# Spreading a batch's preparation between half tiles of attention, a joint gate product, and a plain first layer for the fifth expert

## The chip, the cores and the metric

The kernel runs on one core of a Trainium2 chip. The metric is the device time of one execution in microseconds. The time before is the median of three runs.

## The reference

An attention without softmax is followed by a mixture of experts with balanced capacity.

```python
kv  = einsum('bhsd,bhse->bhde', k, v)          # 8 batches, 8 heads, 576 rows, 64 columns
out = einsum('bhsd,bhde->bhse', q, kv)
x   = out / sqrt(mean(out*out, -1) + 1e-6) * g_norm   # then to (4608, 512)
logits = x @ w_gate                            # 8 experts
# greedy: pairs (token, expert) in falling order of logit, 576 tokens for each expert
h = maximum(x[mask] @ w1[e], 0)                # 512 -> 1024
out[mask] = h @ w2[e]                          # 1024 -> 512
```

Everything is float32. Which tokens an expert gets is only known once all logits are there and the search for the cut has run.

## The kernel before, in words

**Attention.** Eight batches run one after the other. `prepare(b)` is a generator that makes a batch ready: it multiplies k and v (`kv_ps`, L326), turns q with TensorE transposes (`turn_q`, L312, four at a time into `qt`), adds the two halves of the product (`odd`, L332 on ScalarE, then `kv`, L334 on VectorE), and joins to each head's 64 x 64 product 8 columns that give the gate's logits (`kvx`). For the gate it transposes `kv` (`t_ps`, L345), copies it out of PSUM (`kvt`, L347, ScalarE), multiplies it with the scaled gate weights (`w_ps`, L353, once for each half of the partitions) and copies the result into `kvx` (L355). At its end it issues the six loads of the batch after the next (L87, on SP's queue, paced to three under way).

`tiles()` works through a batch in tiles of 128 rows, four for an even batch and five for an odd one. A tile is 8 products in 16 instructions (`o_ps`, L388), two evictions on ScalarE (`sq` L394, `o_sb` L395) and a sum on VectorE (`ms`, L396). At the end of a batch the norm is worked out, the logits go to `lg` and GpSimd scales the rows (`xo`, L415), which SP writes out to `x_dram`.

The order on TensorE, VectorE, ScalarE and SP is that of the program (`manual_schedule`). A loop takes one part of `prepare(b + 1)` after each tile of batch b, and whatever is left after the last tile but one or the last. `prepare` has five parts: kv product of head pair 0 with a turn, the same for pair 1, pairs 2 and 3 together with the additions, turn and `kvt`, and turn, `w_ps`, turn and loads. `early_piece()` puts pieces of the expert search's opening work on VectorE beside the tiles. The transposes, `t_ps` and `w_ps` share two PSUM buffers (tag `tr`); `o_ps` has two of its own.

**Experts.** The eight experts are served one after the other, t = 0 to 7. While expert t is computed, VectorE searches for the tokens of the next ones (`threshold`, `assign`, `fetch`, `control`). The generator `layers(t)` yields the estimated TensorE time of each product, and a loop counts it down to decide where the search's next piece goes. `fetch(t)` isn't started before expert t - 2 is done.

The second layer always uses seven products of quarter matrices in place of eight, with sums made on GpSimd (`column_sums` L915, `sums` L929). For the first layer there are two ways. The plain one (L951) does 64 products with `xt` and `w1`. The other, `first_layer` (L894), does seven products for eight too; it needs sums of weights on GpSimd (`unit_sums`, L855), sums of tokens on VectorE (`token_sums`, L842), and additions of partial results on VectorE (L868, L872). Which experts take it is a tuple:

```python
BOTH = (E - 4, E - 3, E - 2, E - 1)
both = t + 1 in BOTH
turns = {(n, 7) for n in range(1, 6)} if both else {(6, 6)} if t == 0 else {(6, 3)}
```

`turns` says where in the second layer of expert t the tokens of expert t + 1 are transposed (L815): all five blocks there if t + 1 is in `BOTH`; otherwise two there and three in the plain first layer that follows.

Of the kernel before, what the change touches and what calls it, by code (L numbers as in the profile page):

```python
# [7 lines left out]
FT = mybir.dt.float32  # L8
# [7 lines left out]
P = 128  # L16
# [9 lines left out]
def kernel(  # L26
# [272 lines left out]
    def prepare(b):  # L299

        k_sb, v_sb = loaded.pop(("k", b)), loaded.pop(("v", b))

        q_sb = loaded.pop(("q", b)).rearrange("p r j d -> p (r j d)")
        NT = NP * R // 2
        qt = att.tile([P, 2, NT, HP], FT, name="qt", tag="qt", bufs=3)
        turned_q[b] = qt

        def turn_q(n):
            m = min(4, NT - 4 * n)
            t_ps = psa.tile([P, 4, P], FT, name="qt_ps", tag="tr", bufs=2)  # L310
            for x in range(m):
                nc.tensor.transpose(t_ps[:, x, :], q_sb[:, (4 * n + x) * P:(4 * n + x + 1) * P], ident)  # L312

            to, got = qt[:, :, 4 * n:4 * n + m], t_ps[:, 0:m].rearrange("p x (l c) -> p l x c", l=2)
            if n in (1, 2):
                nc.vector.tensor_copy(to, got)
            else:
                nc.scalar.copy(to, got)


        kv_ps = psa.tile([P, 2, 512], FT, name="kv_ps", tag="kv")
        for r in range(NP):
            for j in range(R):
                for l in range(2):
                    ls, cs = slice(l * D, (l + 1) * D), slice(j % 2 * D, (j % 2 + 1) * D)
                    nc.tensor.matmul(kv_ps[cs, l, r * D:(r + 1) * D], lhsT=k_sb[ls, r, j, :], rhs=v_sb[ls, r, j, :],  # L326
                                     start=(j < 2), stop=(j >= R - 2))
            if r < 2:
                turn_q(r)
                yield  # L330
        odd = att.tile([D, 2, NP * D], FT, name="odd", tag="odd")
        nc.scalar.copy(odd, kv_ps[D:P, :, 0:NP * D])  # L332
        kv = att.tile([D, NP, 2, D], FT, name="kv", tag="kv")
        nc.vector.tensor_tensor(kv.rearrange("p r l d -> p l r d"),  # L334
                                kv_ps[0:D, :, 0:NP * D].rearrange("p l (r d) -> p l r d", d=D),
                                odd.rearrange("p l (r d) -> p l r d", d=D), op=AL.add)

        kvx = att.tile([P, H, W], FT, name="kvx", tag="kvx", bufs=3)
        for n in range(2):
            nc.gpsimd.tensor_copy(kvx[n * D:(n + 1) * D, :, 0:D], kv.rearrange("p r l d -> p (r l) d"))  # L340
        yield
        turn_q(2)
        t_ps = psa.tile([P, NP, D], FT, name="t_ps", tag="tr", bufs=2)
        for r in range(NP):
            nc.tensor.transpose(t_ps[:, r, :], kv[:, r].rearrange("p l d -> p (l d)"), ident[0:D, 0:D])  # L345
        kvt = att.tile([P, NP, D], FT, name="kvt", tag="kvt")
        nc.scalar.copy(kvt, t_ps)  # L347
        yield
        turn_q(3)
        w_ps = psa.tile([P, NP, 2 * E], FT, name="w_ps", tag="tr", bufs=2)  # L350
        for r in range(NP):
            for n in range(2):
                nc.tensor.matmul(w_ps[n * D:(n + 1) * D, r], lhsT=kvt[:, r, :],  # L353
                                 rhs=gw[:, r].rearrange("p l e -> p (l e)"), start=True, stop=True)
        nc.vector.tensor_copy(kvx[:, :, D:W], w_ps.rearrange("p r (l e) -> p (r l) e", l=2))  # L355
        kv_of[b] = kvx
        turn_q(4)
        if b + 2 < B:
            for h in range(2):
                for name in "kvq":  # L360
                    load(name, b + 2, h)
# [5 lines left out]
    def tiles(c0, rows):  # L367


        T = len(rows)  # L370
        o_sb = att.tile([P, T, H, W], FT, name="o_sb", tag="o_sb", bufs=2)
        xo = att.tile([P, T, H, D], FT, name="xo", tag="xo", bufs=LAG + 1)
        ms = att.tile([P, T * H], FT, name="ms", tag="ms")
        for t, halves in enumerate(rows):


            o_ps = psa.tile([P, 2, 512], FT, name="o_ps", tag="o", bufs=2)
            for r2 in range(NP // 2):
                for l in range(2):
                    for rp in range(2):  # L380
                        r = 2 * r2 + rp
                        at = [slice(h * HP, (h + 1) * HP) for h in range(2)]
                        parts = [(slice(0, P), halves[0], 2)] if halves[0][0] == halves[1][0] else [
                            (at[n], half, 1) for n, half in enumerate(halves)]
                        for rows_at, (bn, j), m in parts:
                            block = R * r + j
                            ks = slice(block % 2 * D, (block % 2 + 1) * D)
                            nc.tensor.matmul(  # L388
                                o_ps[rows_at, rp, (2 * r2 + l) * W:(2 * r2 + l + 1) * W],
                                lhsT=turned_q[bn][ks, l, block // 2:block // 2 + m].rearrange("p x c -> p (x c)"),  # L390
                                rhs=kv_of[bn][ks, 2 * r + l], start=True, stop=True)
            o4 = o_ps[:, :, 0:NP * W].rearrange("p b (h w) -> p b h w", w=W)
            sq = att.tile([P, H, D], FT, name="sq", tag="sq")
            nc.scalar.activation(sq.rearrange("p (b h) d -> p b h d", b=2), o4[:, :, :, 0:D], ACT.Square, scale=D ** -0.5)  # L394
            nc.scalar.copy(o_sb[:, t].rearrange("p (b h) w -> p b (h w)", b=2), o_ps[:, :, 0:NP * W])  # L395
            nc.vector.reduce_sum(out=ms[:, t * H:(t + 1) * H], in_=sq, axis=AXX)  # L396
            yield
        rt = att.tile([P, T * H], FT, name="rt", tag="rt")
        nc.scalar.activation(rt, ms, ACT.Sqrt, bias=eps)
        inv = att.tile([P, T * H], FT, name="inv", tag="inv")  # L400
        nc.vector.reciprocal(inv, rt)

        nc.vector.scalar_tensor_tensor(rt, in0=inv, scalar=-0.5, in1=inv, op0=AL.mult, op1=AL.mult)
        nc.vector.scalar_tensor_tensor(rt, in0=ms, scalar=EPS, in1=rt, op0=AL.add, op1=AL.mult)
        nc.vector.scalar_tensor_tensor(inv, in0=rt, scalar=1.5, in1=inv, op0=AL.add, op1=AL.mult)  # L405
        part = att.tile([P, T * H, E], FT, name="part", tag="part")
        nc.vector.tensor_tensor(
            part, o_sb[:, :, :, D:W].rearrange("p t h e -> p (t h) e"),
            inv.rearrange("p (a o) -> p a o", o=1).to_broadcast([P, T * H, E]), op=AL.mult)
        nc.vector.reduce_sum(out=lg[:, :, c0:c0 + T].rearrange("p e t -> p t e"),  # L410
                             in_=part.rearrange("p (t h) e -> p t e h", t=T), axis=AXX)

        for t in range(T):
            if c0 + T <= last_own:
                nc.gpsimd.tensor_tensor(xo[:, t], o_sb[:, t, :, 0:D],  # L415
                                        inv[:, t * H:(t + 1) * H].rearrange("p (h o) -> p h o", o=1).to_broadcast([P, H, D]),
                                        op=AL.mult)
            else:
                for h in range(H):
                    late.append(lambda t=t, h=h: nc.scalar.mul(xo[:, t, h], o_sb[:, t, h, 0:D],  # L420
                                                               inv[:, t * H + h:t * H + h + 1]))
        for x in range(0, T, 2):
            y = min(x + 2, T)
            writes.append(lambda x=x, y=y: paced(nc.sync.dma_start(
                x_dram[(c0 + x) * P:(c0 + y) * P, :].rearrange("(t p) f -> p t f", p=P),
                xo[:, x:y].rearrange("p t h d -> p t (h d)"))))
# [21 lines left out]
    with tc.manual_schedule(engines={PE, DVE, ACTE, SPE}):  # L448
# [2 lines left out]
        for _ in range(12):  # L451
            nc.tensor.matmul(w_ps, lhsT=ones_b, rhs=wide, start=True, stop=True)
        for n, _ in enumerate(prepare(0)):
            if n == 2:
                scale_gate()
        bound_logits()
        for b in range(B):
            parts = prepare(b + 1) if b + 1 < B else iter(())
            n = 0
            tile_work = work(b)  # L460
            for _ in tile_work:
                next(parts, None)
                early_piece()
                n += 1
                if n == 4 + b % 2 and b + 1 < B:
                    for _ in parts:
                        pass
            while b + 2 >= B and earlies:
                early_piece()
            for do in late:  # L470
# [358 lines left out]
    FH, TH, DH = FC // 2, (NB - 1) // 2 * P, DM // 2  # L829


    BOTH = (E - 4, E - 3, E - 2, E - 1)
    sums_of = {}

    def token_sums(t):
# [275 lines left out]
```

## Time and profile before

| | us |
|---|---|
| median of 3 runs | 683.48 |
| lowest and highest | 682.77, 684.42 |
| the profiled execution | 683.48 |
| its span | 681.3 |
| PE busy in the span | 624.6 |
| DVE busy in the span | 451.7 |
| ACT, POOL busy | 173.8, 336.2 |
| mean granted TensorE clock | 0.938 |

PE is TensorE, PEld its weight loads, DVE VectorE, ACT ScalarE, POOL GpSimd, SP the queue that issues the loads. The page cuts the span into 40 slices of 17 us; in its rows of digits each one is a tenth (9 is 90% or more), and PEclk is the clock granted to TensorE. In a table of stages each row is a stretch, its length, the busy time and number of instructions of each engine, the clock, the share of the DMA engines and GB/s. In a list of waits a row says who waited for whom, the total in us, how often, and the longest. A `ps` in a name is a PSUM tile.

The attention takes the stretch up to about 121 us, the first search runs from there to 160 us, and the experts from 166 us to the end.

### The profile page before, as it was taken

The numbers are of one execution on the slowest core, as the hardware profiler recorded it, in microseconds if no ns is written. First come the engines' busy times: TensorE is split into PE (matmuls) and PEld (weight loads), VectorE is DVE, ScalarE is ACT, GpSimd is POOL, SyncE is SP. The second block draws the span as 40 slices with busy tenths as digits, with TensorE's granted clock in tenths as the row PEclk, the third lists the DMA queues.
The fourth block names the chain that finished last, engine by engine and source line by source line (L and its number), as shares of the span: only waits on it lengthen the run. The fifth ranks groups of instructions, "written<-read, shape, count | busy, mean of one in ns | idle before, by whom it ended". The sixth has DMA issues, their size and how long they took to land.

```text
span 681.3 us, 12850 instructions
## 1 busy us (share of the span) xinstructions
PE 624.6 (92%) x4994; PEld 487.5 (72%) x4995; DVE 451.7 (66%) x1449; ACT 173.8 (26%) x372; POOL 336.2 (49%) x335
## 2 busy tenths in 40 slices
PE   6999998337999999999999999987989999999994
PEld 4887877233878777877786788656857867786882
DVE  4436778887788888898888786788884056233311
ACT  1436666701210221022102211221113113212200
POOL 1024545002544456355607572785289659938622
PEclk8559999557999999999999999999999999999998
DMA  8978998306307306225207404700190334001001
GB/s 277 307 254 282 310 307 336 150 17 198 118 1 273 111 4 241 76 70 212 106 0 246 142 2 148 232 8 0 46 322 20 125 121 142 1 15 55 1 0 69
DMA packets 41404, 91.02 MB, mean 134 GB/s; under 512 B 3456, under 2 KB 3456, under 8 KB 41344
## 3 DMA queue, kind: packets, MB, share of 16 engines
q1 hardware_dynamic: 34752, 71.31, 30.2%
q0 software_dynamic: 5888, 18.88, 8.3%
q8 instruction: 39, 0.64, 0.4%
q14 instruction: 21, 0.17, 0.1%
q10 hardware_dynamic: 704, 0.02, 0.1%
HBM read 71.32 MB, written 18.87 MB: 132 GB/s over the span
## 4 chain that ended last, share of the span: by engine, by line
PE 76%; DVE 11%; POOL 3%; issue 3%; DMA 3%; ACT 2%; POOLq 0%; DVEq 0%; ACTq 0%; SPq 0%
PE y_ps L1001 27%; PE h_ps L951 17%; PE h_ps L894 9%; PE o_ps L388 5%; PE kv_ps L326 3%; PE y_ps L1016 3%; PE qt_ps L312 3%; PE t_ps L815 3%; DMA k_sb<-in_k_dram 2%; PE given_ps L538 1%; PE given_ps L534 1%; POOL tw L915 1%; PE warm_ps L690 1%; POOL out_dram L822 1%; DMA out_dram<-y_sb,outs 1%
## 5 line engine op out<-in xcount | busy, mean ns | idle before, releaser
L951 PE MATMUL h_ps<-xt,w_sb 128*128 128x256 f32 (+1 forms) x512 | 133.8, 412 | 0.1
L951 PEld LDWEIGHTS h_ps<-xt,w_sb 128*128 128x128 f32 x512 | 93.9, 190 | 25.8 <-issue 3.1
L1001 PE MATMUL y_ps<-tw,sh 128*128 128x256 f32 x384 | 87.4, 381 | 0.0
L1001 PEld LDWEIGHTS y_ps<-tw,sh 128*128 128x128 f32 x384 | 71.4, 190 | 8.9
L742 POOL DMA_INDIRECT xg<-x_dram,ids x40 | 38.2, 956 | 67.4 <-DVE held_ps L658 40.0
L929 POOL TENSOR_TENSOR sh<-hid 128x512 f32<-128x512 f32 x32 | 40.6, 1269 | 52.1 <-ACT hid L954 34.6
L818 ACT ACTIVATE xt<-t_ps,g_col 128x512 f32<-128x512 f32 (+1 forms) x40 | 25.8, 646 | 144.0 <-PE t_ps L815 113.0
L1001 PE MATMUL y_ps<-w_sb,hid 128*128 128x256 f32 x256 | 57.8, 381 | 3.4 <-DVE u L872 3.4
L264 DVE TENSOR_TENSOR over<-mx,held_ps 128x1152 bf16<-128x1152 f32 x42 | 56.9, 1354 | 1.6 <-DVE held_ps L269 0.2
L1001 PEld LDWEIGHTS y_ps<-w_sb,hid 128*128 128x128 f32 x256 | 48.1, 190 | 10.8 <-DVE u L872 3.9
L822 POOL DMA_INDIRECT out_dram<-y_sb,outs x32 | 33.2, 1038 | 43.0 <-DVE u L971 20.7
L894 PE MATMUL h_ps<-sx,tv 128*128 128x288 f32 x192 | 53.1, 410 | 1.0 <-POOL tv L855 0.7
L954 ACT ACTIVATE hid<-h_ps 128x256 f32<-128x256 f32 (+1 forms) x64 | 26.3, 411 | 104.0 <-PE h_ps L951 99.7
L869 ACT ACTIVATE hid<-hid 128x288 f32<-128x288 f32 x64 | 28.2, 445 | 89.1 <-DVE hid L868 86.4
L415 POOL TENSOR_TENSOR xo<-o_sb,inv 128x512 f32<-128x512 f32 x31 | 33.0, 1095 | 28.6 <-DVE inv L405 20.6
L978 POOL TENSOR_TENSOR y_sb<-u,u 128x512 f32<-128x512 f32 x8 | 10.1, 1269 | 72.7 <-issue 49.3
L388 PE MATMUL o_ps<-kvx,qt 64*128 64x72 f32 (+1 forms) x640 | 44.6, 297 | 1.3 <-ACT o_sb L395 1.2
L915 POOL TENSOR_TENSOR tw<-w_sb 128x512 f32<-128x512 f32 x32 | 40.0, 1272 | 11.2 <-DMA w_sb<-in_moe_w_dram 11.0
L388 PEld LDWEIGHTS o_ps<-kvx,qt 64*128 64x128 f32 (+1 forms) x640 | 39.0, 202 | 7.0 <-issue 3.8
L894 PEld LDWEIGHTS h_ps<-sx,tv 128*128 128x128 f32 x192 | 35.8, 190 | 11.2 <-POOL tv L855 1.6
L580 DVE SCALAR_TENSOR_TENSOR held_ps<-n_full,held_ps 32x64 f32<-32x64 f32 x168 | 37.7, 224 | 5.8
L894 PE MATMUL h_ps<-xt,w_sb 128*128 128x288 f32 x128 | 37.1, 412 | 2.8 <-DVE hid L868 2.8
(230 smaller groups left out, 1107.9 us busy)
## 6 DMA issues: line engine op xcount, KB each, us to landing
w_sb<-in_moe_w_dram SPq DMA_DIRECT2D x16, 1024.0 KB, 6.1
w_sb<-in_moe_w_dram SPq DMA_DIRECT2D x8, 2048.0 KB, 16.2
k_sb<-in_k_dram SPq DMA_DIRECT2D x16, 576.0 KB, 5.4
v_sb<-in_v_dram SPq DMA_DIRECT2D x16, 576.0 KB, 6.0
q_sb<-in_q_dram SPq DMA_DIRECT2D x16, 576.0 KB, 6.8
x_dram<-xo SPq DMA_DIRECT2D x16, 512.0 KB, 3.8
x_dram<-xo SPq DMA_DIRECT2D x4, 256.0 KB, 4.1
xg<-x_dram,ids POOLq DMA_INDIRECT x40
```

What stands on the lines that cost most here:

```text
L264: nc.vector.tensor_tensor(over[:, c0:c1], mx[:, c0:c1].rearrange("p (c o) -> p c o", o=1).to_broadcast([P, c1 - c0, NCAND]), cand[:, 1:NCA ...
L388: nc.tensor.matmul(o_ps[rows_at, rp, (2 * r2 + l) * W:(2 * r2 + l + 1) * W], lhsT=turned_q[bn][ks, l, block // 2:block // 2 + m].rearrange ...
L415: nc.gpsimd.tensor_tensor(xo[:, t], o_sb[:, t, :, 0:D], inv[:, t * H:(t + 1) * H].rearrange("p (h o) -> p h o", o=1).to_broadcast([P, H, D ...
L580: nc.vector.scalar_tensor_tensor(some[g * QP:(g + 1) * QP], in0=n_full.to_broadcast([QP, 2 * QP]), scalar=0.5, in1=one_more, op0=AL.is_gt, ...
L742: tokens = nc.gpsimd.indirect_dma_start(out=xg[0:nr], out_offset=None, in_=x_dram, in_offset=bass.IndirectOffsetOnAxis(ap=ids[0:nr, n:n + ...
L822: put = nc.gpsimd.indirect_dma_start(out=out, out_offset=bass.IndirectOffsetOnAxis(ap=ids_of[t][0:nr, n:n + 1], axis=0), in_=y_sb[0:nr, :] ...
L869: nc.scalar.activation(hid[:, f, cs], hid[:, f, cs], ACT.Relu)
L894: nc.tensor.matmul(p_ps, lhsT=left[:, d], rhs=right[:, d], start=d == 0, stop=d == 1)
L915: in_order(nc.gpsimd.tensor_tensor(o[:, m:m + 2], x[:, m:m + 2], y[:, m:m + 2], op=AL.subtract))
L929: in_order(nc.gpsimd.tensor_tensor(o[:, ms], x[:, ms], y[:, ms], op=op))
L951: nc.tensor.matmul(h_ps, lhsT=w1[:, 2 * (d % 2) + d // 2, f * P:(f + 1) * P], rhs=xt[:, d, cs], start=(d == 0), stop=(d == DC - 1))
L1001: nc.tensor.matmul(p_ps[:, n], lhsT=left[:, f, n * P:(n + 1) * P], rhs=right[:, f], start=(f == 0), stop=(f == FH - 1))
```

## The change

`prepare` gets seven parts: head pairs 2 and 3 are parted, and the last turn with the loads stands by itself. A tile yields after its first half too, so that parts can go between halves: at steps 0, 1, 2, 3, 5, 6, 7 of eight in an even batch and at 0, 1, 3, 4, 6, 8, 9 of ten in an odd one. `early_piece` is still called once for each tile. For the gate, `kvt` is copied twice side by side (one buffer instead of two), so that one product gives both halves of the partitions. And expert t = 4 is taken out of `BOTH`: its first layer is the plain one.

```diff
@@ prepare
             if r < 2:
                 turn_q(r)
+            if r + 1 < NP:
                 yield
...
-        kvt = att.tile([P, NP, D], FT, name="kvt", tag="kvt")
-        nc.scalar.copy(kvt, t_ps)
+        kvt = att.tile([P, NP, 2, D], FT, name="kvt", tag="kvt", bufs=1)
+        nc.scalar.copy(kvt, t_ps.rearrange("p r (o d) -> p r o d", o=1).to_broadcast([P, NP, 2, D]))
         yield
         turn_q(3)
         w_ps = psa.tile([P, NP, 2 * E], FT, name="w_ps", tag="tr", bufs=2)
         for r in range(NP):
-            for n in range(2):
-                nc.tensor.matmul(w_ps[n * D:(n + 1) * D, r], lhsT=kvt[:, r, :],
-                                 rhs=gw[:, r].rearrange("p l e -> p (l e)"), start=True, stop=True)
+            nc.tensor.matmul(w_ps[:, r], lhsT=kvt[:, r].rearrange("p n d -> p (n d)"),
+                             rhs=gw[:, r].rearrange("p l e -> p (l e)"), start=True, stop=True)
         nc.vector.tensor_copy(kvx[:, :, D:W], w_ps.rearrange("p r (l e) -> p (r l) e", l=2))
         kv_of[b] = kvx
+        yield
         turn_q(4)
@@ tiles
+                if r2 == 0:
+                    yield
@@ the loop over batches
         for n, _ in enumerate(prepare(0)):
-            if n == 2:
+            if n == 4:
                 scale_gate()
...
-            n = 0
-            tile_work = work(b)
-            for _ in tile_work:
-                next(parts, None)
-                early_piece()
-                n += 1
-                if n == 4 + b % 2 and b + 1 < B:
-                    for _ in parts:
-                        pass
+            for n, _ in enumerate(work(b)):
+                if n in ((0, 1, 3, 4, 6, 8, 9) if b % 2 else (0, 1, 2, 3, 5, 6, 7)):
+                    next(parts, None)
+                if n % 2:
+                    early_piece()
+            for _ in parts:
+                pass
@@ experts
-    BOTH = (E - 4, E - 3, E - 2, E - 1)
+    BOTH = (E - 3, E - 2, E - 1)
```

## The prediction

> **What bounds the kernel now.** I read the page's head first, then its slices, then stages.
>
> ```profile
> span 681.3 us, 12850 instructions
> ...
> PE 624.6 (92%) x4994; PEld 487.5 (72%) x4995; DVE 451.7 (66%) x1449; ACT 173.8 (26%) x372; POOL 336.2 (49%) x335
> ...
> PEclk8559999557999999999999999999999999999998
> ```
>
> PE is busy 92% of the span, so time is won by less PE work, fewer PE waits, or a faster PE clock. The third line shows that the clock is not always full: slices 2 and 3 (17 to 51 us) run at half of it although PE never rests there. That is the attention, whose batches I cut out of the PE timeline by their first o_ps product: batch 0 takes 19.15 to 37.94 us (18.8), batch 1 to 55.31 (17.4), then 11.4, 11.8, 11.4, 12.2 and 11.6 us for batches 2 to 6. The first two do the same work, at half clock.
>
> Next, the experts. Stages cut at the first h_ps and y_ps products: the third expert's second layer is the row from 332.34, the fourth's two layers the next two, then the fifth's two (the one whose first layer the change rewrites starts at 428.18).
>
> ```profile
> 332.34:362.62 30.28, 30.28 (x177) 23.75 (x176) 26.24 (x91) 2.98 (x5) 8.24 (x7) 1.00 0.03 10
> 362.62:397.32 34.70, 34.70 (x193) 26.55 (x194) 28.81 (x105) 8.58 (x19) 22.44 (x20) 1.00 0.54 182
> 397.32:428.18 30.86, 30.86 (x171) 24.39 (x170) 20.80 (x62) 4.73 (x8) 16.21 (x17) 1.00 0.26 95
> 428.18:465.58 37.40, 30.27 (x157) 21.92 (x156) 33.59 (x110) 7.54 (x18) 26.10 (x26) 1.00 0.32 99
> ```
>
> Columns: stretch, its length, busy PE, PEld, DVE, ACT, POOL, then clock and DMA. The fifth expert's first layer is the only one here with PE idle: 37.40 long, 30.27 busy. DVE is busy 33.59 of it. Who held PE, in that stretch and in the attention (19 to 121 us):
>
> ```profile
> PE y_ps L1001 <- DVE u L872: 3.4, 1, 3.4
> PE h_ps L894 <- DVE hid L868: 1.2, 2, 0.9
> PE given_ps L538 <- DVE over L264: 1.1, 2, 0.7
> ...
> PE qt_ps L312 <- ACT kvt L347: 2.0, 4, 0.5
> PE qt_ps L312 <- DVE kvx L355: 1.2, 3, 0.4
> PE o_ps L388 <- ACT o_sb L395: 1.2, 2, 0.8
> ```
>
> So DVE, which does the search and the seven-product layer's additions together, bounds the fifth expert's first layer. The attention loses only 3.2 us to the gate's chain; its clock costs far more.
>
> [...] from shares of half clock in 1.7 us stretches, the flips fall at 9.66, 13.05, 19.9 and 50.6 us, distances of 1, 2 and 9 windows of 3.41. [...] The busy table cut at those windows, all of PE:
>
> ```profile
> 9.66:13.07 3.41, 3.41 (x48) 0.50 1.02 371
> ...
> 19.90:23.31 3.41, 3.41 (x54) 0.50 0.94 314
> ...
> 43.79:47.21 3.42, 3.42 (x52) 0.50 0.91 309
> 47.21:50.62 3.41, 3.41 (x84) 0.50 0.31 113
> 50.62:54.03 3.41, 3.41 (x66) 1.00 0.56 184
> ```
>
> All are full, yet only the first and the 47.21 one were followed by full clock. The same table for the kv_ps products (L326) alone:
>
> ```profile
> 9.66:13.07 3.41, 1.49 (x40) 0.50 1.02 371
> 19.90:23.31 3.41, 1.33 (x36) 0.50 0.94 314
> 26.73:30.14 3.41, 1.27 (x46) 0.50 0.87 262
> 30.14:33.55 3.41, 1.13 (x38) 0.50 0.95 341
> 43.79:47.21 3.42, 1.33 (x36) 0.50 0.91 309
> 47.21:50.62 3.41, 2.32 (x72) 0.50 0.31 113
> ```
>
> [...] A block of 16 o_ps products (one tile, 1.91 us cold) seems to count little[...]. That is my reading, not a shown fact.
>
> **The change part by part.**
>
> *Expert 5 (index 4) goes back to the plain first layer.* PE: removed 7 x 4 x 2 products of 288 columns, the same as the last expert's, 27.4 us (616.25 to 643.61). Added 64 products in 128 instructions: 64 at 216 ns (16 take 3.46) and 64 at 275 ns (16 take 4.40), 31.4 us. So PE work grows by 4.0. DVE loses 16 x 455 + 12 x 452 ns = 12.7 us there and 4 x 0.75 of sx in the stage ahead; POOL loses 16 x 0.73 = 11.7. The stage becomes 30.27 + 4.0 = 34.3 against 37.40: -3.1. Second way: two turning transposes instead of five stay in the layer ahead, so the pair becomes what the third and fourth experts show, 30.28 + 34.70 = 64.98, against 30.86 + 37.40 = 68.26: -3.3. I take -3.2, bounds -4.2 and -2. The search can't run further ahead: its fetch waits until the previous expert is done, so the sixth expert's start, with its own wait of 1.9 us, stays.
>
> *Gate's part.* 16 w_ps instructions (0.64 us) become 8 with weights of 128 columns, at the o_ps price (1.05/16 = 66 ns) 0.53: -0.1 for each of 8 batches, -0.9. kvt's copy doubles to 512 columns: 384 to about 590 ns, the qt row's mean. ACT is 7.2 of 11.4 us busy, so the 0.2 is hidden unless PE stands behind it. One kvt buffer is enough: its reader was a batch ago.
>
> *Spreading.* Five parts become seven, between half tiles. Splitting kv_ps 72 into 36 + 36 costs 2 x 0.73 - 1.31 = 0.15 a batch, +1.0. The kvt and kvx waits (3.2 us) now have half a tile (0.53 us) behind them. But in even batches the last kv_ps part follows the eviction of a whole tile after only 0.66 us, so ACT reaches odd 0.6 us later (sq 0.60 + o_sb 0.63), DVE's kv add (0.68) follows, and t_ps waits an estimated 0.4; behind it in ACT's order stand that tile's sq and the kvt copy. I count half of the waits gone, -1.6. Loads and their order on SP stay: turn_q(4) and the six loads still come after the last tile, POOL's kvx copies a part earlier. early_piece still runs once a tile; the gate's scaling still stands ahead of w_ps. Sum of the two: -1.5, bounds -4 and +2.
>
> *The clock.* At half clock the new order is half tile (0.95 us), kv_ps (1.26), turn (1.04), twice; then half, kv_ps, half, kv_ps. Put from 19.25 us (the first batch starts 0.1 later through kvt), windows hold kv_ps work of: 19.90 to 23.31, about 1.41 us; 23.31 to 26.73, 1.42; 26.73 to 30.14, 1.85. If kv_ps is what counts, the third passes surely (1.85 over 1.49), the first two may. If transposes count nearly fully and o_ps half, the bound lies between 2.66 and 2.85 of 3.41, the first two windows reach 2.74, and the third 2.63: about even. Full clock from 26.7 instead of 50.6 saves 23.9 x 0.43 = 10.2 us (o_ps 1.91 to 1.05, kv_ps 1.26 to 0.73, turn 1.04 to 0.59: 43%); from 23.3, 11.7; from 30.1, 8.8. The loads stand this: in 90 to 101 us they go out every 1.5 us, 48 of them and five early writes are 80 us, and the latest batch would need its own by about 95.
>
> Sum: -3.2 - 1.5 - 10.2 = -14.9. The profiled execution took 683.48 us with a span of 681.3, and is itself the median; so 668.5.
>
> **Rivals.**
> 1. *Clock opens at about the old moment.* Then -4.7: 678.8. For it: the windows' phase may differ by execution. Chance 0.12. With the rise up to one batch later it is within 0.2% (which is about what a measurement can tell from no change): 0.05.
> 2. *Slower: the clock stays low for batches.* The old order had one dense block, 72 kv_ps in a row (2.33 us cold), [...]. The new one cuts it by half a tile, so a window can hold both only if aligned to some 0.2 us. Each further cold batch costs 6 to 7 us (18 against 11.6); from about one such batch on the 4.7 us are used up. Two give 692, all five about 711. Against it: the first batches' windows above. Chance 0.23.
> 3. *Expert 5 gains nothing*: PE +4.0 with the waits kept, if DVE's search alone held PE. Without the additions DVE has 33.6 - 12.7 = 21 us in 34, and the fourth expert shows 28.8 of 34.7 with no wait. It would give 675.5 on top of the early clock; contained in the range.
> 4. *Loads bind once PE is faster*: two or three waits of 1 us in batches 1 to 3, 671. In the range too.
>
> **Numbers.** Early clock 0.60 (665 to 672), old moment 0.12, within 0.05, late 0.23. Faster 0.72, same 0.05, slower 0.23. The range 664 to 692 leaves out the late cases of more than two batches (about 0.11) and little below.
>
> **What would show it.** Right: PEclk at 9 or more from the third slice on, no kvt wait on PE, 8 w_ps instructions a batch, batch 1 in about 12 us, the first search starting near 110 us, and the fifth expert's first layer in 34 to 35 us with PE full. Wrong: 5s in PEclk beyond slice 3 (rival 2), the same two 5s as before (rival 1), or PE waits on L868 or L872 in the fifth expert.

## The result and the profile after

The changed kernel takes 727.61 us (median of four executions, 721.97 to 730.20) against 683.12 (678.14 to 684.42): ratio 1.0654, interval 1.0565 to 1.0744. It is slower by some 44 us where 15 less were forecast. Ratios in this text compare the faster executions of each kernel, ranges are of all.

The page after, the same lines as before the change (span, busy time, PEclk):

```profile
span 728.3 us, 12691 instructions
...
PE 681.7 (94%) x4946; PEld 539.4 (74%) x4947; DVE 437.5 (60%) x1417; ACT 174.8 (24%) x368; POOL 324.1 (44%) x319
...
PEclk9555555555569999999999999999999999999998
```

48 PE instructions fewer, and yet 57 us more of PE busy time: PEclk says why. The clock granted to TensorE is at half from 18.6 to 213.2 us, which is the whole attention and the first search. Before, it came back at 50.6 us and fell again only at 118.9, near the attention's end. The batches of the changed kernel, cut at their first o_ps product (columns as in the stage table of the prediction):

```profile
18.50:38.46 19.96, 19.96 (x239) 17.21 (x239) 7.34 (x28) 7.74 (x15) 1.22 (x2) 0.50 0.92 298
...
59.69:79.75 20.06, 20.06 (x240) 17.31 (x239) 7.17 (x14) 7.42 (x16) 6.48 (x7) 0.50 0.52 178
79.75:100.97 21.22, 21.22 (x271) 18.32 (x270) 7.69 (x15) 8.51 (x17) 5.41 (x6) 0.50 0.50 168
```

PE is busy in every moment of them, none of the waits on kvt and kvx is left, and a batch takes 20 to 21 us instead of 18.8 and 17.4 (the first two, which ran at half clock before as well) and 11.4 to 12.2 (the others). The first search starts at 171.9 instead of 121.8 us: +50.1. From the first h_ps product to the end it is 511.8 us (216.53 to 728.3) instead of 514.5: -2.8. The search between them is 0.3 shorter. Together +47.0, the difference of the spans.

The experts' part of the change did what it was priced at, less a wait. Fourth expert's second layer, then the fifth's first:

```profile
446.60:476.78 30.18, 30.18 (x160) 23.59 (x158) 18.43 (x60) 2.99 (x5) 10.17 (x9) 1.00 0.27 102
476.78:513.10 36.32, 34.78 (x195) 26.58 (x194) 27.19 (x98) 8.58 (x19) 20.48 (x18) 1.00 0.30 97
```

66.50 us against 68.26. Here one wait of 1.5 us is left (given_ps on DVE's over, L264); in a run below it is 0.7.

### The profile page after: what moved, and what is told of

It reads as the page before. It is cut to its first block, busy times and chain, and to the rows that moved or that the text cites. A ratio compares the mean times of both kernels' runs of the same rounds, so it can differ in the third digit from the quotient of the medians.

```text
span 728.3 us, 12691 instructions
## 1 busy us (share of the span) xinstructions
PE 681.7 (94%) x4946; PEld 539.4 (74%) x4947; DVE 437.5 (60%) x1417; ACT 174.8 (24%) x368; POOL 324.1 (44%) x319
## 4 chain that ended last, share of the span: by engine, by line
PE 85%; DVE 7%; POOL 3%; issue 2%; DMA 2%; ACT 0%; POOLq 0%; SPq 0%; DVEq 0%
PE y_ps L1004 26%; PE h_ps L954 20%; PE o_ps L390 9%; PE h_ps L897 8%; PE kv_ps L326 5%; PE qt_ps L312 5%; PE y_ps L1019 4%; PE t_ps L818 2%; PE w_ps L354 2%; DMA v_sb<-in_v_dram 2%; PE given_ps L541 1%; PE given_ps L537 1%; POOL tw L918 1%; PE warm_ps L693 1%; POOL xg L745 1%
## 5 line engine op out<-in xcount | busy, mean ns | idle before, releaser
L954 PE MATMUL h_ps<-xt,w_sb 128*128 128x256 f32 (+1 forms) x640 | 167.1, 412 | 0.1
L954 PEld LDWEIGHTS h_ps<-xt,w_sb 128*128 128x128 f32 x640 | 117.4, 190 | 32.3 <-issue 3.9
L390 PE MATMUL o_ps<-kvx,qt 64*128 64x72 f32 (+1 forms) x640 | 76.0, 410 | 0.0
L390 PEld LDWEIGHTS o_ps<-kvx,qt 64*128 64x128 f32 (+1 forms) x640 | 65.3, 301 | 9.4 <-issue 7.0
L957 ACT ACTIVATE hid<-h_ps 128x256 f32<-128x256 f32 (+1 forms) x80 | 32.9, 412 | 132.4 <-PE h_ps L954 127.1
L264 DVE TENSOR_TENSOR over<-mx,held_ps 128x1152 bf16<-128x1152 f32 x42 | 56.9, 1354 | 1.6 <-DVE held_ps L269 0.2
L400 DVE TENSOR_REDUCE ms<-sq 128x8 f32<-128x512 f32 x36 | 24.5, 685 | 46.3 <-ACT sq L398 46.3
L981 POOL TENSOR_TENSOR y_sb<-u,u 128x512 f32<-128x512 f32 x8 | 10.2, 1270 | 78.4 <-issue 62.9
L326 PE MATMUL kv_ps<-v_sb,k_sb 64*64 64x64 f32 x1152 | 40.2, 305 | 2.1 <-DMA v_sb<-in_v_dram 2.1
L312 PE MATMUL qt_ps<-ident,q_sb 128*128 128x128 f32 x144 | 39.1, 417 | 2.0 <-DMA q_sb<-in_q_dram 1.5
L897 PE MATMUL h_ps<-sx,tv 128*128 128x288 f32 x144 | 39.5, 409 | 0.7 <-POOL tv L858 0.7
```

The source lines that it names most:

```text
L264: nc.vector.tensor_tensor(over[:, c0:c1], mx[:, c0:c1].rearrange("p (c o) -> p c o", o=1).to_broadcast([P, c1 - c0, NCAND]), cand[:, 1:NCA ...
L390: nc.tensor.matmul(o_ps[rows_at, rp, (2 * r2 + l) * W:(2 * r2 + l + 1) * W], lhsT=turned_q[bn][ks, l, block // 2:block // 2 + m].rearrange ...
L897: nc.tensor.matmul(p_ps, lhsT=left[:, d], rhs=right[:, d], start=d == 0, stop=d == 1)
L954: nc.tensor.matmul(h_ps, lhsT=w1[:, 2 * (d % 2) + d // 2, f * P:(f + 1) * P], rhs=xt[:, d, cs], start=(d == 0), stop=(d == DC - 1))
L957: nc.scalar.activation(hid[:, f, cs], h_ps, ACT.Relu)
```

## The experiments

A window is, as in the prediction, one stretch of 3.41 us, counted from a moment at which the granted clock changed. In these traces the changes lie whole numbers of such stretches apart: 57 in the changed kernel (18.64 and 213.2 us), 2, 26 and 16 in h2_half (8.50, 15.32, 104.07 and 158.68 us).

The theory formed on this result (A): the clock comes back to full only after a window that holds a dense block of kv_ps products, as the one from 47.21 us did before (72 products, 2.32 us; those beside o_ps that were followed by half clock held 1.33 us at most), and the split of the 72 into 36 + 36 with half a tile between them took that block away; an order that has full clock keeps it. The rivals: the half tiles or the new gate products keep the clock at half by themselves (B, D); the new order loses even a full clock (C); the order's own waits or the loads lengthen the attention and the clock follows (E). These are my readings, put to the runs.

**1. The block put back in the changed kernel (e1_pair).**

```diff
-            if r + 1 < NP:
+            if r < 2:
                 yield
...
-                if n in ((0, 1, 3, 4, 6, 8, 9) if b % 2 else (0, 1, 2, 3, 5, 6, 7)):
+                if n in ((0, 1, 4, 6, 8, 9) if b % 2 else (0, 1, 3, 5, 6, 7)):
```

> The changed kernel with one thing undone: head pairs 2 and 3 stay together in one part (72 kv_ps products in a row, six parts instead of seven); half tiles, joint gate product and plain fifth expert stay. Theory A [...]: full clock comes back in some batch, the attention ends 10 to 45 us earlier than in the changed kernel, 682 to 715 us in all, depending on which batch's block falls inside a window. Rival B (half tiles or the wider w_ps products keep the clock down, whatever the block): PEclk stays at 5 through the attention, 720 to 730 us.

Measured: 672.8 to 709.4, median 679.7, ratio to before 0.983 (0.965 to 1.000). The clock comes back. The windows of 3.41 us of this run, all of PE:

```profile
23.13:26.55 3.42, 3.42 (x52) 0.50 1.02 373
26.55:29.96 3.41, 3.41 (x84) 0.50 0.90 297
29.96:33.38 3.42, 3.13 (x40) 1.00 0.90 282
57.27:60.68 3.41, 3.13 (x36) 1.00 0.97 296
60.68:64.09 3.41, 3.41 (x54) 0.50 0.94 325
67.51:70.92 3.41, 3.41 (x84) 0.50 0.97 343
70.92:74.33 3.41, 3.41 (x64) 1.00 0.66 196
```

and the kv_ps products alone, first in e1_pair, then in the changed kernel at its own windows:

```profile
19.72:23.13 3.41, 1.33 (x36) 0.50 0.82 263
23.13:26.55 3.42, 1.33 (x36) 0.50 1.02 373
26.55:29.96 3.41, 2.29 (x72) 0.50 0.90 297
67.51:70.92 3.41, 1.88 (x68) 0.50 0.97 343
```

```profile
18.64:22.05 3.41, 1.33 (x36) 0.50 0.93 288
25.47:28.88 3.41, 1.69 (x48) 0.50 0.91 266
66.42:69.84 3.42, 1.37 (x40) 0.50 0.44 158
148.35:151.76 3.41, 1.33 (x36) 0.50 0.80 311
```

A window with 68 or 72 kv_ps products was followed by full clock (the next row); one with 48 beside o_ps was not. In the changed kernel's attention none of 42 windows was (18.64 to 162.0 us); none held more than these 48. The rows at 57.27 and 60.68 show the other direction: after a window at full clock with 4 kv_ps products (the rest are turns, w_ps and o_ps) the clock was at half, although PE was busy for 3.13 of its 3.41 us. Rival B as the whole cause falls.

**2. The fifth expert alone (e2_moe, and the same kernel once more as e2_again).**

```diff
-    BOTH = (E - 4, E - 3, E - 2, E - 1)
+    BOTH = (E - 3, E - 2, E - 1)
```

> The kernel before with only the fifth expert's first layer made plain. If the prediction's step on the experts is right: -2.8 to -3.5 us against the kernel before, 679.5 to 680.5, with the fifth expert's first layer 34 to 35 us long and no PE wait on L868 or L872 in it, and the attention unchanged. If the step is wrong (PE work of +4.0 us with the wait kept): 684 to 687.

Measured: 671.6 to 679.8, ratio 0.982 (0.970 to 0.995). Fourth expert's second layer, fifth's first:

```profile
389.33:419.17 29.84, 29.84 (x160) 23.40 (x158) 18.13 (x59) 2.98 (x5) 10.15 (x9) 1.00 0.29 104
419.17:454.58 35.41, 34.70 (x195) 26.49 (x194) 27.11 (x98) 8.56 (x19) 20.50 (x18) 1.00 0.31 99
```

65.25 against 68.26: -3.0, and from the first h_ps product to the end 510.8 against 514.5. The rest of what the median gains (11.5 us against the 683.1 of before) is the clock: in the profiled execution it is full from 14.1 to 68.7 us with nothing changed in the attention. The kernel before spreads in the same way. Over the 21 executions of it beside the experiments it took from 677.8 us (mean clock 0.948) to 696.4 (0.927), which the median of three before had not shown. The profiles show the windows at another place in each execution; that this alone makes the spread is likely, not shown.

> The kernel before with the plain fifth expert once more, beside the dummies on the same chip. [...] 671 to 680, and 2.8 to 3.5 us below the kernel before where both have the same mean clock.

Measured: 672.0 to 686.6, ratio 0.988 (0.978 to 0.997).

**3. The clock kept full at the start (e3_fill, e4_fill_old).** The same dummy products in the changed kernel and in e2_moe, in `prepare(0)` only:

```diff
+    def fill(b, times):
+        if b == 0:
+            f_ps = psa.tile([P, 2, 512], FT, name="fill_ps", tag="o", bufs=2)
+            for _ in range(times):
+                nc.tensor.matmul(f_ps[:, 0], lhsT=ones_b, rhs=wide, start=True, stop=True)
...
+        fill(b, 4)      # ahead of t_ps; also 6 and 3 in the kv_ps loop, 3 ahead of turn_q(3) and of turn_q(4)
```

> The changed kernel with idle moments of the first prepare filled by 19 dummy bf16 products (128 x 512 ones, into o_ps buffers that are not yet in use)[...]. Theory A [...]: clock full through the attention, batches of 11.5 to 12 us, 664 to 672 us. Rival C (the new order is too thin for full clock at all [...]): falls to half clock within the first batches, over 715 us.

Measured: 723.8 to 730.4, ratio 1.060 (1.048 to 1.072). Theory A's second half is wrong and rival C right: the new order doesn't keep the full clock. It fell at 32.9 us, after a window of 17 o_ps, 6 transposes, 8 w_ps and 8 kv_ps products, and didn't rise again in the attention:

```profile
26.05:29.46 3.41, 3.22 (x70) 1.00 0.85 265
29.46:32.87 3.41, 3.19 (x39) 1.00 0.93 329
32.87:36.28 3.41, 3.41 (x56) 0.50 0.87 274
```

> The kernel before with the plain fifth expert and the same 19 dummy products in the first prepare. Theory A: the first two batches also run at full clock, 30.7 us at half clock x 0.43 = 13 us less, and 3.3 us from the experts: 664 to 670 us. Beside the changed kernel with dummies it shows what spreading, split and joint gate product do at full clock: by the forecast's sums the spread order is up to 1.5 us faster; by the w_ps row of the changed kernel (8 products take 1.06 us where 16 took 0.64) and the split it is 0 to 3 us slower. Rival: the loads of batches 2 and 3 can't keep up, 672 to 677.

Measured: 669.7 to 680.3, ratio 0.983 (0.967 to 0.999). The old order stays at full clock to 95 us, so the same start is kept by one order and lost by the other. It gains no more than e2_moe. Part of the reason is that PE now waits for loads of v, which it doesn't in e2_moe's trace (18 to 125 us):

```profile
PE kv_ps L332 <- DMA v_sb<-in_v_dram: 4.9, 4, 2.1
```

**4. Which part: gate product or spreading (f1_gate, f3_joint, f4_half).** f1_gate is the changed kernel with kvt and w_ps as before; f3_joint is e2_moe with the joint gate product; f4_half is e1_pair with kvt and w_ps as before. The lines exchanged are those of the diff of the change.

> The changed kernel with the gate's product as before (kvt copied once, 16 w_ps products of 64 columns). Theory A [...]: half clock through the attention still; at half clock 16 old products took 0.97 us and the 8 new ones 1.66, so 8 x 0.7 = 5.5 us less than the changed kernel, 717 to 724. Rival D (the slow new w_ps products thin out the windows [...]): full clock comes back, 670 to 700.

Measured: 673.4, 688.9, 724.3 and 727.7. Neither theory alone: with the old w_ps full clock lasted from 14.6 to 79.4 us in the profiled execution, but once at half it was not full again in the attention; in the profile of no run that has the split, and no dummies beside the tiles, was it. Its kv_ps products by window (each row and the one after it are at half clock):

```profile
89.67:93.08 3.41, 2.38 (x72) 0.50 0.97 335
93.08:96.50 3.42, 0.28 (x8) 0.50 0.98 327
110.15:113.56 3.41, 2.04 (x60) 0.50 0.93 355
```

The window from 89.67 held both halves of the split block with half a tile between them, 72 products as in the windows that were followed by full clock, and the clock stayed at half. So it isn't only that the split spreads the block over two windows; a count of kv_ps products in a window doesn't tell the outcome either. What made this window different is not shown.

> The kernel before with the plain fifth expert and the joint gate product, nothing spread. If the wide w_ps products cost what the changed kernel's trace shows at full clock (1.06 against 0.64 us) and kvt's copy 0.2 us more: 8 x 0.4 to 0.6 = 3 to 5 us above e2_moe when the clock does the same, 674 to 678; with more shut windows (the stretch without kv_ps grows by 0.4 us) up to 690. If the prediction's price (0.53 against 0.64) holds: 670 to 672.

Measured: 675.7 to 688.1, median 682.7, ratio to before 1.000 (0.989 to 1.012). The wide product costs (0.6 us in an even batch, see below). That the clock is at half for longer is not shown: its mean is 0.928 to 0.952, and 0.925 to 0.955 in e2_moe and e2_again.

> The kernel with half tiles and the unbroken kv_ps block (as e1_pair), but the gate's product as before; against e2_moe it differs by the half tiles alone. Theory A: [...] 669 to 682. Rival B (half tiles harm by themselves): above 690.

Measured: 672.4 to 692.7, median 675.9, ratio 0.992 (0.984 to 1.000). Half tiles by themselves do little harm.

The four together, all with the plain fifth expert and half tiles:

| | block of 72 kept | split 36 + 36 |
|---|---|---|
| old w_ps | 672 to 693 | 673 to 728 |
| joint w_ps | 673 to 709 | 722 to 730 |

Both edits feed the same loss. With the split no profile, g1_dummy below apart, shows the clock full again in the attention once it has fallen (at 18.64 us in the changed kernel, 32.9 in e3_fill, 79.4 in f1_gate). That the joint product (0.96 us at full clock, the old one 0.65) does its part by lengthening the stretch of turns, w_ps and o_ps after which the clock fell is my reading of the windows at 57.27 in e1_pair and 29.46 in e3_fill; no run tests this apart.

**5. Work added to the changed kernel (g1_dummy).**

```diff
                 if r2 == 0:
+                    for _ in range(3):
+                        nc.tensor.matmul(o_ps[:, 0, 288:512], lhsT=ones_b, rhs=wide[:, 0:224], start=True, stop=True)
                     yield
```

> The changed kernel with work added: three dummy bf16 products (128 x 224 ones, into columns of o_ps that nothing reads) after each first half tile. Theory A (the clock is the whole loss[...]): although TensorE has 108 more products, 10 us of work at full clock, [...] 680 to 700 us result, 27 to 47 less than the changed kernel. Rival E (the order's own waits or the loads make the attention long, the clock only follows): 735 us or more.

Measured: 680.0 to 686.8, 41 to 48 us below the changed kernel's median, with 108 products more. The page and two batches (odd, even):

```profile
PEclk7799999756999999999999999999999999999998
...
35.40:49.20 13.80, 13.80 (x286) 11.61 (x285) 7.46 (x15) 8.41 (x17) 5.39 (x6) 1.00 0.96 311
49.20:62.20 13.00, 13.00 (x251) 10.74 (x250) 7.00 (x14) 7.33 (x15) 6.47 (x7) 1.00 0.94 317
```

This settles that the loss is the clock: the order, parts and loads are those of the changed kernel, only work is added, the mean granted clock is 0.948 to 0.963 where the changed kernel had 0.862 to 0.877, and the kernel is as fast as the one before beside it (ratio 1.003, 0.994 to 1.011). Rival E falls. What in the added products the clock answers to isn't shown.

**6. Dummies where PE waits (h1_spare, h2_half, h3_fill).** h1_spare is e2_moe with seven dummies a batch, h2_half f4_half with the same, h3_fill adds dummies in the first prepare to h1_spare.

```diff
+        def spare(times):
+            for _ in range(times):
+                nc.tensor.matmul(kv_ps[:, 0, 256:512], lhsT=ones_b, rhs=wide[:, 0:256], start=True, stop=True)
...
+        spare(4)
         turn_q(3)
...
+        spare(3)
         turn_q(4)
```

> The kernel before with the plain fifth expert and seven dummy bf16 products (128 x 256 ones, into columns of kv_ps that nothing reads) a batch, four ahead of turn_q(3) and three ahead of turn_q(4), where PE waits 0.4 to 0.5 us for kvt and kvx anyway. Theory A: [...] 668 to 673 us in nearly every execution, a smaller spread than e2_moe has, and no loss from the dummies. Rival F (the dummies only delay[...]): 675 to 682.

Measured: 669.0 to 677.5, median 672.6, ratio to before 0.980 (0.973 to 0.988).

> f4_half (half tiles, unbroken kv_ps block, old gate product) with the same seven dummies a batch; here PE does not wait at those places, since half a tile stands between, so the dummies cost their 7 x 0.108 = 0.76 us a batch, 5 to 6 us. Theory A: [...] 673 to 677, with a smaller spread than f4_half (672 to 693). [...]

Measured: 672.2 to 678.8, median 676.0, ratio 0.988 (0.980 to 0.997). In its profile the clock is full from 15.3 to 104.1 us. Four of its dummies take 0.45 us, start to start (41.82 to 42.27).

> h1_spare with thirteen more dummies in the idle moments of the first prepare as in e3_fill. Theory A: [...] 667 to 671. If the loads bind at full clock (e4_fill_old showed PE at 0.3 of 1.7 us near 48 us): the same as h1_spare, 668 to 673.

Measured: 671.7 to 677.0, median 675.1, ratio 0.988 (0.981 to 0.996). In its profile the clock is full from 11.5 to 110.5 us, nearly the whole attention, and yet it isn't faster than h1_spare; no wait on a load stands in its list, so the reason is open.

The dummies don't show a gain. Three of the six executions of h1_spare fell into 668 to 673, two above 675. Its spread (8.5 us) is smaller than e2_again's (14.6) and equal to e2_moe's (8.3), the ratios overlap, and the clock still fell in its profile, at 78.8 us. Against the kernel before, the intervals of e2_moe, e2_again and h1_spare all lie below 1.

## Why the prediction was wrong, step by step

- **The clock (forecast -10.2): the step that failed.** That the clock was the largest term was read rightly, and so were the moments at which it changed, whole multiples of 3.41 us apart. What failed is "the third passes surely (1.85 over 1.49)" and with it the 0.60 given to the early rise. The bound of 1.49 us came from the window 9.66 to 13.07, which held 2.1 us of transposes too, and I gave it to kv_ps alone. In the changed kernel a window with 1.69 us of kv_ps (25.47) was followed by half clock. The windows beside o_ps and without dummies that were followed by full clock had 1.88 us and more, but the one with 2.38 us in two halves (f1_gate) was not. And in e1_pair full clock came after a window with 1.33 us of kv_ps, which beside o_ps and without dummies never happened; the rest of it was transposes (kv_ps, then transposes, then all of PE in the next window):

```profile
9.48:12.90 3.42, 1.33 (x36) 0.50 1.03 373
9.48:12.90 3.42, 2.07 (x8) 0.50 1.03 373
12.90:16.31 3.41, 2.44 (x81) 1.00 0.94 281
```

  So no bound in us of kv_ps alone fits these windows. The prediction's bound left the transposes out; here 1.33 us of kv_ps with 2.07 us of transposes were followed by full clock, and 1.33 us with o_ps were not. The prediction named the other reading (transposes nearly fully, o_ps half: "about even"), an estimate as well, and gave it too little weight.
- **The rival.** A shortage of dense work was named as the slower rival and priced up to "about 711" for the case in which all batches stay cold, at 0.23 with a range that left that case out. It should have been the forecast: the view that carried it was already there, the jump from 36 to 72 products in the window before the rise.
- **Its size.** Seven cold batches take 143.8 us in the changed kernel against 94.5 before (19.15 to 113.68): 49 us. The rival's 33 us counted 6 to 7 us for each of five more batches; measured, a batch is 8.5 to 9.5 us longer, since at half clock the new w_ps takes 1.65 us, start to start, where the old took 0.97 (35.13 to 36.78 after, 36.35 to 37.32 before), and two half tiles 2.12 (one is 38.46 to 39.52 after) where a whole one takes 1.92 (37.94 to 39.86 before).
- **"26.7 instead of 50.6".** The old moment was taken as given from one trace. Over executions it moves: 14.1 us in e2_moe, 32.4 in e2_again, 50.6 in the trace of before, with later falls. The two rivals on the rise of the clock needed the old order's own spread, which three times within 1.7 us did not show.
- **Fifth expert (forecast -3.2): right.** -3.0 in e2_moe, -1.8 in the changed kernel's trace with its wait of 1.5 us; PE work 30.27 to 34.70, as summed (34.3). The sixth expert's own wait of 1.9 us stayed, as said.
- **Gate's part (forecast -0.9): wrong sign.** The price was taken from o_ps, whose weights have 64 rows. With 128 rows and 128 columns, 8 products take longer than 16 narrow ones. Changed kernel's first one at full clock, then one at half; below, the one of before:

```profile
16.30 1.06 PE L354 MATMUL w_ps<-gw,kvt 128*128 128x16 f32 x8
...
35.13 1.72 PE L354 MATMUL w_ps<-gw,kvt 128*128 128x16 f32 x8
```

```profile
17.36 0.64 PE L353 MATMUL w_ps<-gw,kvt 128*64 128x16 f32 x16
```

  The nearer row was L951's weight load, 190 ns with 128 x 128. In f3_joint an even batch takes 12.05 us (48.69 to 60.74) against 11.4, where -0.1 was forecast: 0.3 are the products, 0.3 the longer wait for the kvt copy (0.74 instead of 0.46).
- **Spreading (forecast -0.6 after its own costs): the waits go, as forecast, and are spent again.** At full clock two batches of f1_gate take 11.56 and 11.75, 23.31 us, against 11.39 + 11.77 = 23.16 before. The term left out is the half tile itself:

```profile
60.34 1.12 PE L391 MATMUL o_ps<-kvx,qt 64*128 64x72 f32 x16
...
62.11 0.67 PE L391 MATMUL o_ps<-kvx,qt 64*128 64x72 f32 x8
```

  Start to start a half takes 0.60 (62.11 to 62.71 us, where the next kv_ps follows) and a whole 1.04 (60.34 to 61.38): two halves cost 0.16 more than a whole. The half tiles make 7 runs of o_ps of a batch's 4 (even) or 5 (odd), so some 0.3 to 0.5 us a batch (estimate); the waits on kvt and kvx were worth as much, 3.2 us over seven batches.
- **Rival 4, the loads:** they bound in e4_fill_old, with 4.9 us of waits; in h3_fill, at full clock nearly throughout, no wait on a load is listed.

## What to carry to other kernels

A PE row that is full says nothing of its clock (PE is 92% busy before and 94% after): read PEclk first, cut the trace at the moments at which it changes (multiples of 3.41 us apart in these traces), and count what kind of work each stretch holds. An edit that only moves work can lose more by breaking up a dense block than it gains by filling waits: here the block of 72 kept together was worth 48 us in the median (e1_pair against the changed kernel), the waits 3.2. Compare kernels over enough executions to see their spread (677.8 to 696.4 us for the kernel before). A product's price is taken from a row with the same rows and columns of weights: the new w_ps takes 1.06 us where the price from o_ps said 0.53.

## What was not expected of the hardware

The granted clock follows something else than PE's busy time: in the changed kernel it stayed at half over 42 windows in a row, each full of PE work. In the attention of all fourteen profiles, 17 windows at half clock with 68 or more kv_ps products in them were followed by full clock and one was not (f1_gate, 72 in two halves with o_ps between); with 60 or fewer, only windows with 8 transposes (before 9.66, e1_pair 9.48) or with dummies were. What the clock goes by is not shown. Three dummy bf16 products of 224 columns a tile, 0.3 to 0.4 us in g1_dummy's trace (44.74 to 45.04, 40.26 to 40.65), went with full clock from 25.0 to 127.4 us, where the changed kernel's was at half.
